# Sliding-window attention and mixture of experts on one core: narrower score blocks, shifted value copies and a new order for the last three batches

## The chip, the core and the metric

The kernel runs on one core of a Trainium2 chip. The core has TensorE (PE in the profile; its weight loads are PEld), VectorE (DVE), ScalarE (ACT), GpSimd (POOL) and SyncE (SP), each with its own queue of instructions, and 16 DMA engines. The metric is the device time of one launch in microseconds (us), over repeated runs. A profile is one more execution, whose trace has the start and the duration of every instruction. TensorE's clock has two levels, 1.2 and 2.4 GHz; the granted clock is given as a share of the upper one.

## What is computed

```python
# attention: batch 8, heads 8, 576 positions, head size 64
scores = scale * q @ k.T                      # only |query - key| <= 32 counts
attn   = exp(scores) masked to the band, divided by its row sum
x      = attn @ v                             # -> 4608 tokens x 512
# experts: the modality of a token picks its gate bias
e      = argmax(x @ w_gate + modality_bias[modality])
out    = gate_weight * relu(x @ w1[e]) @ w2[e]
```

## The kernel before, in words

Every instruction of the program is placed by a table of steps, `ORDER`. A step has a name, its numbers, the engine that does it (`/v` VectorE, `/a` ScalarE, `/p` GpSimd) and, behind a colon, the banks of the PSUM memory (eight, 0 to 7) that a matmul step writes. The program walks the table once and emits the steps' instructions; each engine then runs its own in that order, and waits on semaphores where a step needs another engine's result or a bank that is still being read.

Attention, for batch `b` and group `g` of four heads: `t` transposes queries and keys (VectorE). `SA` and `SB` make the scores (TensorE): each matmul multiplies 32 rows of one head, the four heads sit in four row groups of the array, and keys come in blocks of 128 with a window of 192 queries (128 at the end). `SA` has 16 matmuls of 192 columns, `SB` 16 of 192 and 8 of 128. `sa` and `sb` take the exponential into `pt` (ScalarE: one instruction of 1,536 columns, and for `sb` another of 512). `M` multiplies by the band's mask (VectorE, 1,920 columns, four per batch). `V` multiplies by the values (18 matmuls of 65 columns per step, four steps per batch; the 65th column is a one, so that the row sum comes out beside the result), and `v` divides by that sum (VectorE: a reciprocal and a multiply). `lv` loads values (GpSimd).

Then `X` sorts the tokens of a block by expert with a one-hot matrix (`G` makes it), `pa` and `pb` append them to two lists (ScalarE). `L`, `lo`, `E`, `sm`, `rc` make the gate. `U` is the first layer of a tile of 256 tokens (8 matmuls of 256 columns), `u` its relu, `D` the second layer (4 matmuls of 512 columns per half), `y` the scaling by the gate, `O` the scattered store (GpSimd). Tile 18 takes the tokens that are left over, with weights that `Wx` copies. `c0` to `c17` check on the device that the assumptions on the lists held; `c17` loads the resulting flag into a register of every engine, and a branch then skips a slow general path.

Names that matter below, with the lines of the profile: scores L687, exponentials L695 and L698, mask L712, values L729, `v` L743 and L758, `U` L916, `D` L942, `u` L931 and L933, `y` L956 and L958, `O` L965, checks L995 to L1032, the branch L1215.

Of the kernel before, what the change touches and what calls it, by code (L numbers as in the profile page):

```python
# [23 lines left out]
BF16 = mybir.dt.bfloat16  # L24
# [40 lines left out]
u7.0/a U6.1:0 v17/v u6.2/a U7.1:7 u6.1/a lo3/v t5.1.1/v E3/a V16:12 u7.1/a SB5.0:3456 v16/v l7.0.2/p D6.0.0:7 sb5.0/a
t6.1.1/v V19:01 U7.3:2 sm3/v lv7.1/p v19/v SA5.0:3456 u7.3/v D6.0.1 O5.1/p sa5.0/a e10/v t6.0.0/v X4.2:2 X4.0:0 U7.2:1
lv6.1/p rc3/v pa4.0/a t6.0.1/v pb4.0/a X4.1:3 D7.0.0:4 u7.2/a M20/v pb4.1/a D7.0.1 pa4.1/a pb4.2/a X4.3:3 pa4.2/a
D6.1.0:6 y7.0/v pb4.3/a y6.0/v pa4.3/a O7.0/p D6.1.1 M21/v SB5.1:0123 V20:45 y6.1/v sb5.1/a U9.1:7 v20/v O6.1/p L4:6
V21:45 l7.1.2/p lo4/v SA6.0:0123 E4/a O6.0/p sm4/v D7.1.0:6 v21/v sa6.0/a D7.1.1 rc4/v t6.1.0/v u9.1/a U9.0:4 y7.1/a
t7.0.0/v SA5.1:0123 u9.0/a O7.1/p U8.1:6 sa5.1/a U9.2:7 u8.1/a U9.3:4 M22/v u9.2/a SB6.0:0123 u9.3/a M23/v U8.0:7  # L70
sb6.0/a V22:45 U8.3:6 v22/v u8.0/a V23:01 e13/v SA6.1:2345 v23/v U8.2:7 sa6.1/a M24/v X4.4:0 D9.1.0:1 pb4.4/a c2/v
u8.2/v D9.1.1 pa4.4/a X5.0:7 X5.1:0 y9.1/v X5.2:2 pb5.0/a V24:34 pa5.0/a G6/v O9.1/p pb5.1/a X5.3:1 D8.0.0:7 pa5.1/a
v24/v pb5.2/a D9.0.0:0 pa5.2/a t7.1.0/v u8.3/a SB6.1:2345 pb5.3/a pa5.3/a M25/v D9.0.1 sb6.1/a U11.1:1 t7.1.1/v D8.0.1
y9.0/v u11.1/a M26/v U10.2:2 O9.0/p y8.0/a U10.0:6 M27/v lv7.0/p V25:01 u10.2/a V26:34 v25/v X5.4:2 D8.1.0:7 pa5.4/a
v26/v u10.0/a D8.1.1 pb5.4/a SA7.1:0123 y8.1/v V27:45 t7.0.1/v O8.1/p U11.3:7 sa7.1/a v27/v U10.1:6 Wx u11.3/a
SB7.1:0123 c3/v G7/v u10.1/a U11.2:7 sb7.1/a X6.0:6 L5:4 U10.3:5 lo5/v E5/a pb6.0/a U11.0:0 pa6.0/a u10.3/v Jy12/v
X6.1:6 D10.0.0:5 u11.0/v pa6.1/a sm5/v u11.2/a M30/v SB7.0:0123 pb6.1/a D10.0.1 rc5/v sb7.0/a X6.2:7 D11.1.0:4 y10.0/v
M31/v O10.0/p D11.0.0:5 pb6.2/a pa6.2/a SA7.0:0123 O8.0/p D11.1.1 sa7.0/a D11.0.1 y11.1/a U12.0:7 M29/v y11.0/a X6.3:1
U12.1:0 M28/v V29:56 u12.1/a L6:4 u12.0/a U13.0:2 pa6.3/a lo6/v E6/a sm6/v U12.2:4 u13.0/a rc6/v v29/v pb6.3/a U13.3:0
# [5 lines left out]
u14.3/v u16.3/a L9:0 D14.0.0:3 E8/a lo9/v N/p c6/v O11.0/p U14.2:0 c7/v c8/v sm8/v D14.1.0:6 rc8/v u14.2/a U16.2:5 E9/a
sm9/v c9/v u15.1/v D14.1.1 u16.2/a D14.0.1 y14.1/a D16.1.0:5 O14.1/p U17.1:6 D16.1.1 u17.1/v c10/v U17.3:7 y16.1/a c11/v
c12/v y14.0/a D15.0.0:6 O16.1/p c13/v u17.3/v D16.0.0:3 O14.0/p U15.3:7 D16.0.1 u15.3/a U17.0:5 D15.0.1 u17.0/v c14:7
U17.2:0 c15/v y15.0/v D15.1.0:7 y16.0/v u17.2/a O15.0/p D15.1.1 O16.0/p D17.1.0:0 y15.1/v c16/v D17.1.1 O15.1/p
D17.0.0:7 U18.1:3 U18.0:6 u18.1/v D17.0.1 u18.0/a y17.1/v D18.0.0:6 y17.0/v O17.1/p rc9/v D18.0.1 y18.0/a c17 O17.0/p
O18.0/p  # L90
"""


@with_exitstack
def kernel(
    ctx: ExitStack,
    tc: tile.TileContext,
    q: bass.AP,
    k: bass.AP,
    v: bass.AP,  # L100
# [41 lines left out]
    RB = 2
# [1105 lines left out]
```

## Time and profile before

| what | us |
|---|---|
| runs (3) | 208.20, 208.52, 210.06; median 208.52 |
| profiled execution, its own time | 210.04 |
| its span, first to last instruction | 208.3 |
| PE busy in the span | 195.7 (94%) |
| DVE, ACT, POOL busy | 152.2, 131.4, 97.3 |
| PE from 98.44 to 200.50 | 102.06 busy of 102.06 |
| last store issued, and span's end | 201.99, 208.3 |

Busy time is the time in which an engine has an instruction in work. TensorE's instructions overlap one another, so how often it starts one says more than how long one takes. A wait is put down to what ended it.

### The profile page before, as it was taken

Reading aid. Unit: us, or ns where it says so; the run is one execution under the profiler, and the core shown is the slowest. Engines: PE = TensorE matmul, PEld = TensorE weight load, DVE = VectorE, ACT = ScalarE, POOL = GpSimd, SP = SyncE. Lnnn points to the kernel's source line nnn. Section 1 sums busy time; section 2 is a strip of 40 time slices with the busy share of each in tenths; the row PEclk is TensorE's granted clock in tenths of the full one; section 3 lists DMA queues with packets and bytes.
Section 4 is the critical chain, followed back from the end, with each engine's and each line's share of the span. In section 5 each row is a group of like instructions: output and inputs, shape, how many; then the busy total and the mean of one; then the engine's idle time right before and its main releaser. Section 6 shows DMA issues by size and latency. Waiting matters only on the chain. (4 is left out here: it accounts for less than half of the span.)

```text
span 208.3 us, 6244 instructions
## 1 busy us (share of the span) xinstructions
PE 195.7 (94%) x2583; PEld 140.3 (67%) x2583; DVE 152.2 (73%) x304; ACT 131.4 (63%) x223; POOL 97.3 (47%) x137
## 2 busy tenths in 40 slices
PE   7997998999999989999999999999999999999950
PEld 5766787777666677669657876777597669656520
DVE  3598999999889978899998679976566334542330
ACT  6097794778877986976778969678751732431120
POOL 7987851695089888145545102510501152122550
PEclk9999999999999999999999999999999999999996
DMA  4999999999999999989696911192200132112330
GB/s 66 206 174 183 212 209 196 211 213 192 201 193 268 171 253 235 208 174 169 97 185 129 318 75 50 55 199 112 102 5 0 53 151 105 50 50 104 138 118 8
DMA packets 47661, 30.41 MB, mean 146 GB/s; under 512 B 38883, under 2 KB 38923, under 8 KB 47371
## 3 DMA queue, kind: packets, MB, share of 16 engines
q0 software_dynamic: 46608, 27.79, 83.4%
q1 hardware_dynamic: 1019, 2.16, 2.9%
q8 instruction: 22, 0.36, 0.7%
q14 instruction: 12, 0.10, 0.1%
HBM read 36.76 MB, written 9.70 MB: 223 GB/s over the span
## 5 line engine op out<-in xcount | busy, mean ns | idle before, releaser
L965 POOL DMA_INDIRECT out_dram<-ys,ids x37 | 41.2, 1112 | 85.9 <-DVE ys L958 45.8
L916 PE MATMUL banks<-XT,w_sb 128*128 128x256 bf16 x576 | 71.2, 273 | 0.7 <-DVE xt L758 0.7
L942 PE MATMUL banks<-w_sb,hT 128*128 128x512 bf16 x288 | 69.5, 379 | 0.0
L916 PEld LDWEIGHTS <-w_sb 128*128 128x128 bf16 x576 | 53.8, 98 | 11.4 <-issue 1.8
L695 ACT ACTIVATE pt<-banks 128x1536 bf16<-128x1536 f32 x32 | 46.6, 1458 | 13.0 <-PE banks L687 9.8
L933 ACT ACTIVATE hT<-banks 128x512 bf16<-128x512 f32 x57 | 33.0, 598 | 30.1 <-PE banks L916 27.9
L942 PEld LDWEIGHTS <-hT 128*128 128x128 bf16 x296 | 26.9, 98 | 26.3 <-issue 0.8
L655 DVE STREAM_TRANSPOSE qk<-qk 128x576 int32<-128x576 int32 x32 | 38.4, 1244 | 2.1 <-DMA qk<-in_k_dram 1.8
L712 DVE TENSOR_TENSOR pt<-pt,mask 128x1920 bf16<-128x1920 bf16 x28 | 31.5, 1148 | 4.0 <-ACT pt L695 4.0
L758 DVE TENSOR_TENSOR xt<-banks,recs 128x640 bf16<-128x640 f32 x32 | 26.4, 824 | 1.1
L729 PE MATMUL banks<-vt,pt 128*128 128x65 bf16 x576 | 22.4, 193 | 1.4 <-DMA vt<-in_v_dram 0.6
L729 PEld LDWEIGHTS <-pt 128*128 128x128 bf16 x576 | 21.0, 97 | 4.0 <-issue 1.4
L798 ACT CAST XT<-banks 128x352 f32 (+3 forms) x40 | 17.9, 448 | 5.1 <-PE banks L778 4.6
L231 POOL DMA_DIRECT2D vt<-in_v_dram x16 | 20.2, 1270 | 1.3 <-PE banks L729 1.3
L958 DVE TENSOR_SCALAR ys<-banks,Gt 128x512 f32<-128x512 f32 x20 | 14.5, 739 | 7.8 <-PE banks L942 7.8
L931 DVE TENSOR_SCALAR hT<-banks 128x512 bf16<-128x512 f32 x17 | 11.6, 685 | 11.7 <-PE banks L916 11.6
L956 ACT ACTIVATE ys<-banks,Gt 128x512 f32<-128x512 f32 x17 | 11.5, 699 | 12.6 <-PE banks L942 12.6
L687 PE MATMUL banks<-qk 32*128 32x192 bf16 (+1 forms) x640 | 18.5, 239 | 0.1
L812 ACT CAST XT<-banks 128x352 f32 (+2 forms) x39 | 17.6, 451 | 1.2 <-PE banks L778 0.9
L687 PEld LDWEIGHTS <-qk 32*128 32x128 bf16 x640 | 12.2, 92 | 7.3 <-issue 6.2
L974 PE MATMUL banks<-zero_b 128*128 128x256 bf16 x86 | 13.8, 318 | 2.0 <-DVE zero_b L320 1.5
L778 PE MATMUL banks<-oh,xt 128*128 128x128 bf16 (+1 forms) x160 | 12.3, 214 | 0.3 <-DVE xt L758 0.3
(159 smaller groups left out, 143.6 us busy)
## 6 DMA issues: line engine op xcount, KB each, us to landing
vt<-in_v_dram POOLq DMA_DIRECT2D x16, 288.0 KB, 6.7
w_sb<-in_moe_w_dram POOLq DMA_DIRECT2D x4, 1024.0 KB, 14.0
qk<-in_q_dram POOLq DMA_DIRECT2D x6, 576.0 KB, 10.7
qk<-in_k_dram POOLq DMA_DIRECT2D x6, 576.0 KB, 6.8
wx<-w_sb SPq DMA_DIRECT2D x2, 1024.0 KB, 6.1
qk<-in_q_dram POOLq DMA_DIRECT2D x4, 288.0 KB, 7.7
qk<-in_k_dram POOLq DMA_DIRECT2D x4, 288.0 KB
out_dram<-ys,ids POOLq DMA_INDIRECT x37, 2.7
```

The costliest lines, as they stand in the source:

```text
L231: nc.gpsimd.dma_start(v_t[b % NV][:, n_ * i:n_ * i + n_, 0:D], v[b].rearrange("h s d -> (h s) d").rearrange("(n p) d -> p n d", p=P)[:, n_ ...
L655: nc.vector.transpose(qk_t[b % 2][:, g, at:at + S].rearrange("p (t r) -> p r t", r=R), Ct["l", b][:, u, g].bitcast(I32).rearrange("p (r j) ...
L687: nc.tensor.matmul(st[:, h, WIN * i_:WIN * i_ + w_], qk[32 * h:32 * h + 32, c_, QK + k0:QK + k0 + P], qk[32 * h:32 * h + 32, c_, q0:q0 + w ...
L695: nc.scalar.activation(pt[:, :, 2 * part:2 * part + 2, 0:WIN], st[:, :, 0:2 * WIN].rearrange("p h (j c) -> p h j c", c=WIN), ACT.Exp, scal ...
L712: nc.vector.tensor_tensor(out=p_ap, in0=p_ap, in1=mask[:], op=ALU.mult)
L729: nc.tensor.matmul(o_ap, pt[:, c1:c1 + P], vt[:, g0 + j, 0:D + 1], start=(m == 0 and i_ == 0), stop=(i_ == len(mine) - 1), skip_group_chec ...
L758: nc.vector.tensor_tensor(out=o_ap, in0=o_v[:, :, :, 0:D], in1=rec.unsqueeze(3).to_broadcast([P, 2, NM, D]), op=ALU.mult)
L798: ins = nc.scalar.copy(XT[:, :, bass.ds(r_, w_)], Ct["X", b, m][:, :, 0:w_])
L916: ins = nc.tensor.matmul(ph[:, u_, :], w1[:, f0:f0 + 2 * P - 1:2], rhs, start=(kd == 0), stop=(kd == n_kd - 1))
L933: nc.scalar.activation(o_ap, i_ap, ACT.Relu)
L942: nc.tensor.matmul(Ct["D", t_, s_], Ct["h", t_][:, kf, P * s_:P * s_ + P], w2, start=(kf == 0), stop=(kf == n_kf - 1))
L965: ins = nc.gpsimd.indirect_dma_start(out=out, out_offset=bass.IndirectOffsetOnAxis(ap=ids[:, u_:u_ + 1], axis=0), in_=Ct["y", t_, s_][:], ...
```

## The change

For batches 5 to 7 (`b >= OLD`):

- Scores. `SA` now has six blocks of 64 queries per head group, 48 matmuls of 64 columns; the two ends of the sequence are in `SE`, once per batch for both groups, 32 matmuls of 96 columns. `SB` is gone.
- Exponentials. `sa` is one instruction of 1,536 columns per group, `se` one of 1,536 per batch.
- Masks. `M` with two numbers covers 1,536 columns per group, `Me` 1,536 per batch. The buffers `pm` and `pe` lie in the two old `pt` buffers; `Kr` and `Kx` set once what stays constant between the blocks.
- Values. Blocks of 64 queries need keys that start at odd multiples of 64. `Vx` copies the values, shifted by 64 rows, into a second tile `vx`: two copies of 64 partitions by 1,122 columns per half batch, on VectorE, and for the first half of batch 6 on ScalarE. `V` has 16 matmuls of 65 columns instead of 18.
- The tile `vx` is also used earlier, in place of another tile (`ohp`), and the column of ones is two wide.
- Order. The table's first 497 entries are the same; behind them all is in another order, and some `u` and `y` steps are on the other of the two engines. `c17` and the last checks stand at the end, behind the last store, where before they stood ahead of the last two stores.

```diff
-l7.0.2/p D6.0.0:7 sb5.0/a ... SB5.0:3456 ... O17.1/p rc9/v D18.0.1 y18.0/a c17 O17.0/p O18.0/p
+Kr0/v V19:45 U7.2:7 Kr1/a u7.2/a SA5.0:0123 sa5.0/a D6.0.0:6 ... D17.1.1 y17.1/a O17.1/p c7/v ... c16/v c17/p
...
+    QW, EW, NW = 64, 96, 6
+    TW, SE = 3 * QW, 256
...
+    def Vx(eng, b, i):
+        n_ = G // 2
+        lo, hi = slice(n_ * i, n_ * i + n_ - 1), slice(n_ * i + 1, n_ * i + n_)
+        for to, from_, at in ((slice(0, 64), slice(64, P), lo), (slice(64, P), slice(0, 64), hi)):
+            o_ap, i_ap = vx_t[to, lo], v_t[b % NV][from_, at]
...
+                copy(eng, o_ap, i_ap)
...
+    def Kr(eng, i):
+        pad(eng, pm_t[i].rearrange("p (j c) -> p j c", c=TW)[:, :, QW:2 * QW])
...
+    def scores(st, at, b, g, k0, q0, w_):
+        qk = qk_t[b % 2][:, g].bitcast(BF16).rearrange("p (t c) -> p c t", c=2)
+        for c_ in range(2):
+            for h in range(4):
+                nc.tensor.matmul(st[:, h, at:at + w_],
+                                 qk[32 * h:32 * h + 32, c_, QK + k0:QK + k0 + P],
+                                 qk[32 * h:32 * h + 32, c_, QP + q0:QP + q0 + w_],
+                                 start=(c_ == 0), stop=(c_ == 1), skip_group_check=True)
...
+    def SA(_, b, g):
...
+        for i in range(NW):
+            scores(Ct["S", b, g], QW * i, b, g, QW * (i + 1), QW * (i + 1) + 32, QW)
...
+    def SE_(_, b, w):
+        Ct["T", b, w] = some_banks()
+        for j, g in enumerate(groups(w)):
+            scores(Ct["T", b, w], 2 * EW * j, b, g, 0, 0, EW)
+            scores(Ct["T", b, w], 2 * EW * j + EW, b, g, S - P, S - EW, EW)
...
+    def Mn(_, b, g):
+        p_ap = pm_t[(NG * b + g) % NPM].rearrange("p (t w c) -> p t w c", w=3, c=QW)[:, :, 0:3:2]
+        m_ap = mask[:, 0:1, 64:P].unsqueeze(1).to_broadcast([P, 2 * NW, 2, QW])
+        nc.vector.tensor_tensor(out=p_ap, in0=p_ap, in1=m_ap, op=ALU.mult)
...
+    def values(it, ot):
...
+            for i_, (m, pt, c1, w, last) in enumerate(runs):
+                n_, odd = divmod(R // 2 * h + w, 2)
+                src = vx_t if odd else v_t[b % NV]
+                nc.tensor.matmul(ot[:, h, (D + 1) * m:(D + 1) * (m + 1)], pt[:, c1:c1 + P],
+                                 src[:, R // 2 * hp + n_, 0:D + 1],
+                                 start=(i_ == 0), stop=last, skip_group_check=True)
```

VectorE between batch 4's last values and batch 5's first ones. In the old kernel this is the work ahead of the step `V20` and the first steps after it (L712 masks, L655 transposes, L958 `y`):

```order
L743 RECIPROCAL recs<-banks 128x10
L758 TENSOR_TENSOR xt_93<-banks,recs 128x2x5x64
L712 TENSOR_TENSOR pt_86<-pt_86,mask 128x10x192
L999 TENSOR_TENSOR sc__150<-sc__150,hn 128x40
L931 TENSOR_SCALAR hT<-banks 128x512
L958 TENSOR_SCALAR ys<-banks,Gt 128x512
L507 TENSOR_TENSOR oh<-iob,col 128x640
L743 RECIPROCAL recs<-banks 128x10
L758 TENSOR_TENSOR xt_91<-banks,recs 128x2x5x64
```

In the changed kernel the same stretch of VectorE, from the last `v` of batch 4 (`xt_93`) on, reads (L335 constants, L643 transposes, L746 and L752 masks, L174 shifted copies, L1027 `y`):

```order
L335 MEMSET pt_87 128x8x32 x2
L941 RECIPROCAL Gt<-sm 128x4
L643 STREAM_TRANSPOSE qk_84<-qk 128x18x32
L746 TENSOR_TENSOR pt_86<-pt_86,mask 128x12x2x64
L643 STREAM_TRANSPOSE qk_84<-qk 128x18x32
L174 COPY vx<-vt_90 64x1122 x2
L1027 TENSOR_SCALAR ys<-banks,Gt 128x512
L752 TENSOR_TENSOR pt_87<-pt_87,mask 128x8x192
L174 COPY vx<-vt_90 64x1122 x2
L1068 TENSOR_TENSOR sc__151<-sc__151,hn 128x40
L812 RECIPROCAL recs<-banks 128x10
L827 TENSOR_TENSOR xt_94<-banks,recs 128x2x5x64
```

Four shifted copies and two transposes of batch 6 now stand ahead of the first `v` of batch 5; the one-hot of L507 and a relu (L931) have moved away.

VectorE at the end of the program, before:

```order
L1016 TENSOR_REDUCE gec<-sc__150 128x37
L1018 SCALAR_TENSOR_TENSOR gec<-gec,vv 128x37
L1020 TENSOR_SCALAR gec,bad<-gec 128x37
L169 CAST badb<-bad 128x3
L931 TENSOR_SCALAR hT<-banks 128x512 x2
L1027 TENSOR_SCALAR fl<-banks 128x3
L958 TENSOR_SCALAR ys<-banks,Gt 128x512 x3
L169 CAST fl_i<-fl 128x1
L931 TENSOR_SCALAR hT<-banks 128x4x128
L958 TENSOR_SCALAR ys<-banks,Gt 128x512 x2
L872 RECIPROCAL Gt<-sm 128x1
L1032 TENSOR_LOAD fl_i
```

And in the changed kernel:

```order
L1027 TENSOR_SCALAR ys<-banks,Gt 128x512
L1077 TENSOR_SCALAR sc__151<-recs 128x320
L1079 SCALAR_TENSOR_TENSOR sc__151,rs<-recs,sc__151 128x320
L1083 TENSOR_SCALAR sc__151<-lo__147 128x296
L1085 TENSOR_REDUCE gec<-sc__151 128x37
L1087 SCALAR_TENSOR_TENSOR gec<-gec,vv 128x37
L1081 TENSOR_SCALAR bad<-rs 128x1
L1089 TENSOR_SCALAR gec,bad<-gec 128x37
L174 CAST badb<-bad 128x3
L1096 TENSOR_SCALAR fl<-banks 128x3
L174 CAST fl_i<-fl 128x1
L1101 TENSOR_LOAD fl_i
```

The checks have moved behind VectorE's last `y`, and every engine's load of the flag comes after all of them.

## Rows read from the trace of the kernel before

**Rows 1.** The page's first part: busy us (share of the span) xinstructions.

```profile
PE 195.7 (94%) x2583; PEld 140.3 (67%) x2583; DVE 152.2 (73%) x304; ACT 131.4 (63%) x223; POOL 97.3 (47%) x137
```

**Rows 2.** Windows, all engines: stretch, its length, busy us (xcount) each, PEclk.

```profile
98.44:200.50 102.06, 102.06 (x1227) 71.12 (x1224) 64.66 (x124) 58.84 (x103) 30.65 (x29) 1.00 0.43 102
```

**Rows 3.** Groups of TensorE, 98.44 to 200.9 us: busy, mean ns | idle before.

```profile
L729 PE MATMUL banks<-vt,pt 128*128 128x65 bf16 x252 | 9.7, 193 | 0.0
L687 PE MATMUL banks<-qk 32*128 32x192 bf16 (+1 forms) x240 | 6.9, 239 | 0.0
```

**Rows 4.** Timeline of TensorE around an old SB step: start us, us.

```profile
117.78 0.38 PE L916 MATMUL banks<-XT,w_sb 128*128 128x256 bf16 x2
118.09 0.63 PE L687 MATMUL banks<-qk 32*128 32x192 bf16 x24
118.66 1.05 PE L916 MATMUL banks<-XT,w_sb 128*128 128x256 bf16 x8
119.54 0.71 PE L729 MATMUL banks<-vt,pt 128*128 128x65 bf16 x18
120.09 1.04 PE L916 MATMUL banks<-XT,w_sb 128*128 128x256 bf16 x8
```

**Rows 5.** The same around an old SA step.

```profile
121.61 0.52 PE L687 MATMUL banks<-qk 32*128 32x192 bf16 x16
122.07 0.61 PE L916 MATMUL banks<-XT,w_sb 128*128 128x256 bf16 x4
```

**Rows 6.** The same around matmuls of 8 columns.

```profile
110.65 0.55 PE L843 MATMUL banks<-wgd,XT 128*128 128x8 bf16 x16
111.11 0.28 PE L729 MATMUL banks<-vt,pt 128*128 128x65 bf16 x4
```

**Rows 7.** Groups of all engines by shape: busy us, mean ns.

```profile
L695 ACT ACTIVATE pt<-banks 128x1536 bf16<-128x1536 f32 x32 | 46.6, 1458 | 13.0 <-PE banks L687 9.8 <-PE banks L729 2.9
...
L712 DVE TENSOR_TENSOR pt<-pt,mask 128x1920 bf16<-128x1920 bf16 x28 | 31.5, 1148 | 4.0 <-ACT pt L695 4.0
...
L958 DVE TENSOR_SCALAR ys<-banks,Gt 128x512 f32<-128x512 f32 x20 | 14.5, 739 | 7.8 <-PE banks L942 7.8
...
L931 DVE TENSOR_SCALAR hT<-banks 128x512 bf16<-128x512 f32 x17 | 11.6, 685 | 11.7 <-PE banks L916 11.6
```

**Rows 8.** The same, nearest rows for the copies.

```profile
L507 DVE TENSOR_TENSOR oh<-iob,col 128x640 bf16<-128x640 bf16 x8 | 6.5, 818 | 0.0
...
L429 DVE TENSOR_SCALAR mask<-neg 128x768 bf16<-128x768 bf16 x2 | 0.6, 332 | 0.0
```

**Rows 9.** Timeline of VectorE where the order parts.

```profile
97.99 1.25 DVE L655 STREAM_TRANSPOSE qk<-qk 128x576 int32<-128x576 int32 x1
99.19 0.22 DVE L743 RECIPROCAL recs<-banks 128x10 f32<-128x10 f32 x1
99.45 0.82 DVE L758 TENSOR_TENSOR xt<-banks,recs 128x640 bf16<-128x640 f32 x1
100.19 1.25 DVE L655 STREAM_TRANSPOSE qk<-qk 128x576 int32<-128x576 int32 x1
```

**Rows 10.** Timeline of all engines at the end.

```profile
198.97 1.90 PE L942 MATMUL banks<-wx,hT 128*128 128x512 bf16 x8
...
200.96 0.69 ACT L956 ACTIVATE ys<-banks,Gt 128x512 f32<-128x512 f32 x1 [2.04 <-PE banks L942]
201.99 0.98 POOL L965 DMA_INDIRECT out_dram<-ys,ids  x1 [0.30 <-ACT ys L956]
```

**Rows 11.** The branch's line and the store's: count, ns min/median/max, first and last start.

```profile
L1215 PEldq COMPARE_BRANCH  x1: 3442/3442/3442, 199.6 to 199.6; - x1
```

**Rows 12.** The value loads' line (L231), its last row.

```profile
DMA to landing us min/median/max: 5.6/6.7/7.9
```

**Rows 13.** Groups of VectorE: the two longest checks.

```profile
L1010 DVE SCALAR_TENSOR_TENSOR sc__150<-recs,sc__150 128x320 f32<-128x320 f32 x1 | 0.5, 491 | 0.0
...
L1016 DVE TENSOR_REDUCE gec<-sc__150 128x37 f32<-128x296 f32 x1 | 0.5, 453 | 0.0
```

More of the change, by code (lines that the diff above doesn't have):

```diff
@@ L65 @@
[L65 to L79, printed above, removed]
@@ L85 @@
[L85 to L89, printed above, removed]
@@ new lines @@
+D7.1.0:5 t6.1.0/v Vx5.0/v y6.0/v u7.3/a D7.0.1 sa5.1/a X4.1:0 X4.2:1 pb4.1/a pa4.1/a y7.0/a O7.0/p l7.0.2/p
+O5.1/p Me5.2/v pb4.2/a Vx5.1/v c2/v V20:23 v20/v t6.0.1/v D7.1.1 y7.1/a t6.0.0/v X4.3:0 V21:67 D6.1.0:2 v21/v
+pa4.2/a pa4.3/a pb4.3/a D6.1.1 y6.1/a U8.2:0 X4.4:1 L4:2 lo4/v U8.3:6 SE6.2:2345 M5.1/v u8.3/v U8.1:7 u8.1/v
+Kx0/a se6.2/a Me6.2/v u8.2/v U9.0:6 V22:23 v22/v U9.2:7 pb4.4/a V23:45 v23/v U9.1:0 O6.0/p lv6.1/p Vx6.0/a
+u9.2/a u9.0/a U8.0:2 SA6.1:4567 pa4.4/a X5.0:1 X5.1:3 u9.1/a D9.1.0:0 E4/a pa5.0/a pa5.1/a pb5.0/a sa6.1/a
@@ new lines @@
+u8.0/v D8.0.0:2 D8.0.1 pb5.1/a Jy12/v t7.1.0/v sm4/v rc4/v SA6.0:4567 D8.1.0:3 D8.1.1 X5.2:1 Vx6.1/v M6.1/v
+sa6.0/a M6.0/v U9.3:4 V27:56 X5.3:7 u9.3/v D9.1.1 y8.0/a y8.1/a pb5.2/a e13/v v27/v pb5.3/a y9.1/v pa5.2/a
+V24:34 v24/v U11.1:5 U11.2:0 G6/v pa5.3/a L5:3 lo5/v u11.2/v V26:67 X5.4:3 v26/v U10.3:4 G7/v lv7.0/p O6.1/p
+V25:01 v25/v u10.3/v O7.1/p u11.1/v pb5.4/a U10.1:2 U10.2:6 U10.0:0 X6.0:4 X6.2:1 u10.2/v pa5.4/a U11.0:5
+X6.1:6 X6.3:7 pa6.0/a u10.0/a pa6.1/a D9.0.0:0 D9.0.1 pb6.0/a u10.1/v pb6.1/a l7.1.2/p t7.1.1/v pb6.2/a U11.3:6
@@ L136 @@
     NV = 3
+    OLD = 5
     PM = (0,1)
@@ L639, in W @@
     @named
-    def W(_, which, i):
+    def W(_, which, i, h=None):
         if ("er", i) not in Ct:
@@ L673, with scores1 @@
     op["MB"] = lambda _, b, g: masked(b, g, 1)
-    def scores(b, g, part):
+    def scores1(b, g, part):
         pm = NG * b + g in PM
@@ new lines, in Me, with M @@
+    @named
+    def Me(_, b, w):
+        p_ap = edges(b, w).rearrange("p g h c -> p (g h) c")[:, :, 32:32 + 2 * EW].rearrange("p h (a c) -> p h a c", a=2)
+        m_ap = mask[:].rearrange("p j c -> p (j c)")[:, 32:32 + 2 * (WIN + 32)].rearrange("p (a c) -> p a c", a=2)
+        nc.vector.tensor_tensor(out=p_ap, in0=p_ap, in1=m_ap[:, :, 0:EW].unsqueeze(1).to_broadcast(list(p_ap.shape)),
+                                op=ALU.mult)
+    @named
+    def M(_, it, g=None):
+        if g is not None:
+            return Mn(_, it, g)
@@ L716, in V @@
         b, hp = divmod(it, NH)
+        ot = some_banks()
+        if b >= OLD:
+            values(it, ot)
+            Ct["V", it] = ot
+            return
         pt, vt = pair(it), v_t[b % NV]
-        ot = some_banks()
         for h in range(2):
```

190 lines of the change are left out of this document (104 added, 86 removed).

## The prediction

> **What bounds the kernel now.** I read the busy shares first, then the windows, then the timeline of the engine that they single out. TensorE is busy 94% of the span, VectorE 73%, ScalarE 63% [rows 1]. An average does not say that TensorE is the limit where the change is, so the window counts. The two orders part at the step `V16`, at 98.44 us. From there to 200.50 TensorE is busy 102.06 of 102.06 us at a granted clock of 1.00 (the 2.4 GHz level), VectorE 64.7 and ScalarE 58.8 [rows 2], and the groups of scores and values were not preceded by any idle time [rows 3]. So in the whole stretch that the change touches nothing but TensorE's own work sets the time. Work taken from the other two engines is worth nothing; a new order can win nothing by removing waits, because there are none, and can only add some. The gain must be TensorE's own time.
>
> **TensorE's scores, priced by sets.** I call four matmuls, one in each row group, a set. An old `SA` has 4 sets of 192 columns and takes 0.46 us to the next step's start (121.61 to 122.07) [rows 5]; `SB` has the same 4 and 2 sets of 128 and takes 0.57 (118.09 to 118.66) [rows 4]. So a set of 128 costs about 56 ns, where 128 columns at 2.4 GHz are 53. The columns set the pace, with some 4 ns on top. Four sets of 192 are then 4 x 84 = 0.34 us, and 0.12 of the 0.46 is for starting and for changing back to full-array work. Entering costs too: two matmuls of `U` start at 117.78, each takes 0.11 (8 in 118.66 to 119.54), so the scores could have started at 118.00 and did at 118.09 [rows 4]. A step so costs 0.55 (`SA`) or 0.66 (`SB`), and three batches 6 x 0.55 + 6 x 0.66 = 7.26 us.
>
> The new `SA` has 12 sets of 64 columns. Followed by columns a set is 27 + 4 = 31 ns, the step 0.37 + 0.12 + 0.09 = 0.58. `SE` has 8 sets of 96: 44 ns each, 0.56. Three batches: 6 x 0.58 + 3 x 0.56 = 5.16. **Gain 2.10 us**, although there are 144 more score matmuls.
>
> No row shows a set of 64. Its bounds: below, the columns (31 ns); above, 57 ns, since the weights that it loads are those of a 128-column set, which shows 56. At 57 for both sizes `SA` is 0.89 and `SE` 0.67, three batches 7.35, a loss of 0.09. I take 31: matmuls of 8 columns, each with its own load of 128 columns, follow each other in 0.46 / 16 = 29 ns in the full array [rows 6], so a load need not take 57.
>
> The Trainium skill speaks against me here. "TensorE: Matmul & The Clock Gate", section "LDWEIGHTS (loading the stationary operand)", prices a load at its columns divided by 1.2 GHz and says that 32 rows take as long as 128. An estimate from that page: 107 ns per load and set, 6 x 1.49 + 3 x 1.07 = 12.2 us of scores, and a kernel some 4 us slower. The sets of 56 ns in this trace exclude that figure; what is left of the rule is my first rival, priced there from rows alone.
>
> **Values.** A `V` step of 18 takes 0.55 us (119.54 to 120.09) [rows 4], 30.6 ns a matmul. 24 fewer: **gain 0.73 us**. The source tile makes no difference.
>
> **ScalarE and VectorE.** Per batch the exponentials go from four instructions of 1.46 us [rows 7] and two short ones to three; that is off the path and counts for nothing. VectorE's masks go from four of 1.15 [rows 7] to three of 1,536 columns, in proportion 0.92. It gets ten shifted copies of 1,122 columns. No row shows one. Nearest below: 768 columns from one bf16 source in 0.33 us [rows 8], in proportion 0.48. Nearest above: a two-source one-hot of 640 columns in 0.82 [rows 8], in proportion 1.43. I take 0.45, since a copy has one source; the other end is my second rival. `Kr` and `Kx` are a few tenths each.
>
> Does that hold TensorE up? I summed both sides at the narrowest places; a VectorE instruction starts 0.08 before the end of the last (100.19 against 99.45 + 0.82) [rows 9], so each counts its row less 0.08.
>
> - Before `V20`, the first new values. VectorE is free at 99.19 [rows 9]; then two `v` of 1.0, `Kr0` 0.4, `Kx1` 0.3, two transposes of 1.17, two masks of 0.87, two copies of 0.4, a `y` of 0.66 and small change: the last mask ends at about 107.5. TensorE's work from `V16` to `V20` sums to 9.5 us, so it arrives at 107.9. Slack 0.4.
> - From the end of `U9.3` to `U10.0`, which needs the bank that `v25` reads: VectorE has three `u` (0.61), four `v` (1.0), a `y` (0.66) and two one-hots (0.74), with small change 7.7 us; TensorE has 8.0. After the time it takes VectorE to see a matmul end, next to nothing is left.
> - GpSimd now issues the second half of batch 6's values behind the store of `y7.0`. That `y` can end at about 109.2 by TensorE's sum, five issues of about 1.0 us [rows 10] come first, so about 115; landing takes 6.7 us [rows 12], and the copy can start at 121.7. The last mask of batch 6 behind it waits for `sa6.0` anyway: its scores end at about 124.0, the exponential takes 1.46, so 125.5. Covered; without that cover it would cost up to 2 us.
>
> The plan is tight, so small excesses will show. **Loss 0.5 us**, with 0 and 1.5 as ends.
>
> **The end.** Before, the last matmuls end at T = 198.97 + 1.90 = 200.87, the last `y` starts at 200.96, its store at 201.99 [rows 10], and the span ends 7.4 us after T. Now the last product is `D17.1`, again with a `y` on ScalarE and one store. Priced at nothing. The checks are new in this place: the last `y` of VectorE can end at T - 0.9, nine checks of at most 0.49 [rows 13] are some 2.3 us, so T + 1.4; a matmul and two more bring the flag at about T + 2.1. TensorE's branch takes 3.44 [rows 11], T + 5.6 with the register load to come. That is still inside the 7.4.
>
> **The sum.** -2.10 - 0.73 + 0.50 = -2.33 us. The profiled span of 208.3 becomes 206.0. The profiled execution itself took 210.04, near the slowest of the three runs; I set the difference against their median, 208.52: **206.2 us**.
>
> **Rivals.**
>
> - *Weight loads set the pace of narrow sets* (57 ns). For: each set loads four times 128 columns, and no row has fewer columns per load in row groups. Against: 29 ns in the full array [rows 6]. Then +0.09 - 0.73 + 0.3 of waits: 208.2 us, no change.
> - *The shifted copies run at the two-source rate*, 1.43 instead of 0.45 each: the kernel becomes slower. A step of two is 1.9 late. Two steps fall ahead of `V20` and of `SE6.2`, where 0.4 to 0.6 are free; batch 6's is covered; two fall ahead of batch 7's values, with slack of 0.5 to 1.0. Four times 1.9 less 2.5 is 5.1 us: 208.52 - 2.33 + 5.1 = 211.3. It decides from about 1.0 us a copy, where the waits eat the gain. Against: one-source bf16 work here is fast [rows 8].
> - *The flag comes last.* If TensorE's branch, now late, outlasts the last store's landing, the end moves by up to 1 us: about 206.9. For: 3.44 us is long [rows 11], and only some 1 us is free. Against: the sum above.
>
> **How the numbers follow.** Forecast 0.62, loads 0.16, copies 0.09, flag 0.09; 0.04 for none of these. The forecast's own span is 205.4 to 207.2 (waits of 0 to 1.5). The loads' case and the flag's must be inside the range, the copies' case need not: 205.3 to 208.7. One per cent is 2.1 us, about what a measurement of this kernel can tell from no change: faster is below 206.4, slower above 210.6. The forecast lies just below the first bound, so it gives 0.41 to faster and 0.21 to no change; the flag's case splits (0.03 and 0.06), loads go to no change, copies mostly to slower (0.07). Rounded, with the rest: faster 0.45, same 0.46, slower 0.09.
>
> **What would show it.** In the changed trace: 48 score matmuls from their first start to the next step in about 0.49 us, 32 in 0.47 (rivals: 0.80 and 0.58); `V` of 16 in 0.49; copies of 64 by 1,122 in 0.4 to 0.5 us; TensorE busy all through, with idle time of some tenths at `V20`, `U10.0` and around; the last matmul's end about 2.3 us earlier, and 7.4 us from there to the end. The forecast is wrong if sets of 64 need over 45 ns, if TensorE idles for more than 1.5 us behind `V16`, or if the stretch behind the last matmul grows.

## The result

The changed kernel took 211.25 us (median of 10, 210.1 to 215.14), the kernel before 208.47 on the same chip (10, 208.2 to 210.06): ratio 1.0116, interval 1.0077 to 1.0154. It is slower by about 1.2%, where I had forecast 206.2 us, and it lies outside the range of 205.3 to 208.7. (Ratios here and below are of undisturbed runs and need not be the quotient of the medians.) The profiled execution took 211.17 us, its span is 209.5. Page part 1 [rows 1] and the window from `V16` to the last matmul [rows 2] of the changed kernel (window: length, busy us of PE, PEld, DVE, ACT, POOL with counts, PEclk, DMA):

```profile
PE 193.1 (92%) x2703; PEld 138.9 (66%) x2703; DVE 154.2 (74%) x317; ACT 126.0 (60%) x216; POOL 94.6 (45%) x137
...
98.44:200.78 102.34, 100.07 (x1345) 69.86 (x1342) 64.83 (x126) 53.48 (x95) 29.09 (x29) 1.00 0.44 102
```

Both kernels reach `V16` at nearly the same time (98.44 us before, 98.33 now). TensorE had no idle time from there to the end before; now it has 2.27 us. What it does is cheaper, as forecast. Timeline of the new `SA` and `SE` steps [rows 4, 5], then groups by shape (busy us, mean ns) for scores, masks and copies [rows 7, 8]:

```profile
100.40 0.55 PE L699 MATMUL banks<-qk 32*128 32x64 bf16 x48
100.88 1.04 PE L1011 MATMUL banks<-w_sb,hT 128*128 128x512 bf16 x4
...
102.72 0.52 PE L699 MATMUL banks<-qk 32*128 32x96 bf16 x32
103.18 1.04 PE L1011 MATMUL banks<-w_sb,hT 128*128 128x512 bf16 x4
```

```profile
L699 PE MATMUL banks<-qk 32*128 32x64 bf16 x288 | 3.6, 189 | 0.5 <-issue 0.5
...
L746 DVE TENSOR_TENSOR pt<-pt,mask 128x1536 bf16<-128x1536 bf16 x6 | 5.6, 953 | 0.5 <-ACT pt L727 0.5
L174 DVE COPY vx<-vt 64x1122 bf16<-64x1122 bf16 x10 | 4.5, 451 | 1.3 <-DMA vt<-in_v_dram 1.2
```

An `SA` of 48 matmuls takes 0.48 us to the next step (forecast 0.49), an `SE` 0.46 (0.47), a `V` of 16 matmuls 0.48 to 0.52 (0.49), a copy 451 ns (0.45).

The time went to two places. First, TensorE stopped. Its waits from 98 us to the last matmul (total, times, longest), and the timeline of the worst stretch:

```profile
PE banks L912 <- issue: 0.8, 2, 0.4
PE banks L699 <- DVE lo__147 L923: 0.7, 1, 0.7
PE banks L699 <- issue: 0.5, 1, 0.5
PE banks L1011 <- ACT ys L1025: 0.3, 1, 0.3
```

```profile
142.10 1.89 PE L1011 MATMUL banks<-w_sb,hT 128*128 128x512 bf16 x8 [0.26 <-ACT ys L1025]
143.92 0.62 PE L699 MATMUL banks<-qk 32*128 32x64 bf16 x45
145.07 0.22 PE L699 MATMUL banks<-qk 32*128 32x64 bf16 x3 [0.52 <-issue]
145.22 0.20 PE L912 MATMUL banks<-wgd,XT 128*128 128x8 bf16 x2
145.78 0.29 PE L912 MATMUL banks<-wgd,XT 128*128 128x8 bf16 x6 [0.36 <-issue]
146.51 0.35 PE L912 MATMUL banks<-wgd,XT 128*128 128x8 bf16 x8 [0.43 <-issue]
```

The 0.3 us behind `ys` are a plain wait for a `y`, which every trace of this order has. "Issue" is time in which the engine waits for nothing that the profile shows. TensorE stops inside the second score step of batch 7 and twice inside batch 6's logits, and starts again at 145.07, 145.78 and 146.51, every 0.7 us. The wait of 0.7 us behind `lo` is of another form: VectorE reads batch 4's logits (`lo`) late.

```profile
112.18 0.82 DVE L827 TENSOR_TENSOR xt<-banks,recs 128x640 bf16<-128x640 f32 x1
114.64 0.19 DVE L923 TENSOR_TENSOR lo__147<-banks,mbd 128x32 f32<-128x32 f32 x1 [1.64 <-PE banks L985]
```

The logits' matmuls end at 113.31 by the record and VectorE is free, yet `lo` starts at 114.64.

Second, the end [rows 10, 11]: last matmuls, last `y`, last store, TensorE's branch, and SyncE's waits at the end.

```profile
199.26 1.89 PE L1011 MATMUL banks<-w_sb,hT 128*128 128x512 bf16 x8
201.54 0.69 ACT L1025 ACTIVATE ys<-banks,Gt 128x512 f32<-128x512 f32 x1 [3.78 <-PE banks L1011]
202.51 0.97 POOL L1034 DMA_INDIRECT out_dram<-ys,ids  x1 [0.60 <-issue]
```

```profile
L1284 PEldq COMPARE_BRANCH  x1: 4562/4562/4562, 203.8 to 203.8; - x1
```

```profile
SPq L1312 <- DMA out_dram<-ys,ids: 2.0, 1, 2.0
SPq L1312 <- PEq L1284: 1.2, 1, 1.2
```

T, the end of the last matmuls, is 201.15, the branch runs to 208.33, the span to 209.5: 8.3 us behind T, where it was 7.4. SyncE has the last store when it still waits 1.2 us for TensorE's branch.

### The profile page after: what moved, and what is told of

Its sections match the earlier page's. It is cut to its first block, busy times and chain, and to the rows that moved or that the text cites. A ratio compares the mean times of both kernels' runs of the same rounds, so it can differ in the third digit from the quotient of the medians.

```text
span 209.5 us, 6485 instructions
## 1 busy us (share of the span) xinstructions
PE 193.1 (92%) x2703; PEld 138.9 (66%) x2703; DVE 154.2 (74%) x317; ACT 126.0 (60%) x216; POOL 94.6 (45%) x137
## 4 chain that ended last, share of the span: by engine, by line
PE 39%; issue 35%; POOL 9%; DVE 6%; ACT 4%; DMA 3%; POOLq 1%; ACTq 0%; DVEq 0%
PE banks L1011 14%; PE banks L985 12%; POOL out_dram L1034 7%; PE banks L675 4%; PE banks L798 4%; DMA qk<-in_q_dram 3%; DVE xt L827 2%; PE banks L847 2%; ACT pt L683 2%; POOL qk L220 1%; PE banks L699 1%; ACT pt L686 1%; PE banks L912 1%; ACT pt L738 1%; POOLq L1039 1%
## 5 line engine op out<-in xcount | busy, mean ns | idle before, releaser
L1002 ACT ACTIVATE hT<-banks 128x512 bf16<-128x512 f32 x49 | 28.6, 599 | 30.7 <-PE banks L985 28.2
L643 DVE STREAM_TRANSPOSE qk<-qk 128x576 int32<-128x576 int32 x32 | 38.3, 1238 | 2.3 <-DMA qk<-in_k_dram 1.7
L683 ACT ACTIVATE pt<-banks 128x1536 bf16<-128x1536 f32 x20 | 29.2, 1461 | 6.6 <-PE banks L675 4.8
L1000 DVE TENSOR_SCALAR hT<-banks 128x512 bf16<-128x512 f32 x25 | 16.7, 685 | 10.3 <-PE banks L985 9.9
L1025 ACT ACTIVATE ys<-banks,Gt 128x512 f32<-128x512 f32 x22 | 15.0, 696 | 10.4 <-PE banks L1011 10.4
L760 DVE TENSOR_TENSOR pt<-pt,mask 128x1920 bf16<-128x1920 bf16 x16 | 18.0, 1151 | 0.1
L798 PEld LDWEIGHTS <-pt 128*128 128x128 bf16 x360 | 13.1, 97 | 3.1 <-issue 1.3
L798 PE MATMUL banks<-vt,pt 128*128 128x65 bf16 x360 | 14.0, 193 | 1.1 <-ACT pt L686 0.4
L1027 DVE TENSOR_SCALAR ys<-banks,Gt 128x512 f32<-128x512 f32 x15 | 11.0, 741 | 3.0 <-PE banks L1011 2.9
L847 PEld LDWEIGHTS <-xt 128*128 128x128 bf16 x160 | 10.2, 98 | 3.6 <-issue 0.5
L675 PE MATMUL banks<-qk 32*128 32x192 bf16 (+1 forms) x400 | 11.6, 239 | 1.1 <-DVE vt L335 1.0
```

What stands on the lines that cost most here:

```text
L643: nc.vector.transpose(qk_t[b % 2][:, g, at:at + S].rearrange("p (t r) -> p r t", r=R), Ct["l", b][:, u, g].bitcast(I32).rearrange("p (r j) ...
L675: nc.tensor.matmul(st[:, h, WIN * i_:WIN * i_ + w_], qk[32 * h:32 * h + 32, c_, QK + k0:QK + k0 + P], qk[32 * h:32 * h + 32, c_, q0:q0 + w ...
L683: nc.scalar.activation(pt[:, :, 2 * part:2 * part + 2, 0:WIN], st[:, :, 0:2 * WIN].rearrange("p h (j c) -> p h j c", c=WIN), ACT.Exp, scal ...
L760: nc.vector.tensor_tensor(out=p_ap, in0=p_ap, in1=mask[:], op=ALU.mult)
L798: nc.tensor.matmul(o_ap, pt[:, c1:c1 + P], vt[:, g0 + j, 0:D + 1], start=(m == 0 and i_ == 0), stop=(i_ == len(mine) - 1), skip_group_chec ...
L847: nc.tensor.matmul(t_[:, kd, :], x_t[b % NX][:, m, P * kd:P * kd + P], Ct["oh", b][:, m, 0:n_], start=True, stop=True, skip_group_check=True)
```

## The experiments

Each set of runs below was on one chip, and the kernel before gives its measure. In three sets (called quiet) it takes 207.5 to 207.6 us, in the other three and in the first measurement (called pausing) 208.5 to 208.9. That the kind of set decides, I learned from the runs. The expectations speak of chips with and without pauses, but that it is the chip is not shown: the record gives the first set, which was quiet, and the fifth, which was pausing, the same chip number, 7.

**First set, quiet (before 207.57).** Three single edits and their sum:

```diff
 e1: checks ahead, flag ahead of the last store
-y18.0/v D17.1.0:6 O15.1/p O18.0/p c6/v D17.1.1 y17.1/a O17.1/p c7/v c9/v ... c14:6 c15/v c16/v c17/p
+rc8/v y16.0/v c6/v c7/v c8/v ... sm9/v c9/v ... c13/v ... D18.0.1 c14:4 y18.0/v ... c15/v c16/v D17.1.1 y17.1/a c17/p O17.1/p
 e2: copies of the last tile's weights later, from ScalarE
-D16.1.1 Wx U18.0:2      r_ = reg(..., [ET.SP], 0, 1)          nc.sync.dma_start(v1, ...)
+u14.3/a Wx D13.0.0:6    r_ = reg(..., [ET.Activation], 0, 1)  nc.scalar.dma_start(v1, ...)
 e3
-L4:2 lo4/v
+L4:7 lo4/v
```

> The changed kernel with its checks moved ahead: the two checks of the value reciprocals and their count stand in VectorE's idle time before the last tile's logits, the four of the logits right behind the last tile's sum, the one-column matmul ahead of the last eight matmuls, the flag's load ahead of the last store. Theory A (the flag is the last thing that TensorE waits for, and its branch, 4562 ns from 203.77 us, outlasts the landing of the last store): the branch starts at about 201 us, the stretch from TensorE's last matmul to the span's end falls from 8.35 to about 7.3 us, and the time by 1.0 to 1.2 us against the changed kernel (211.25 us), to about 210.1. Rival (the store's landing sets the end in both, and the late branch only shows beside it): the time stays within 0.3 us of the changed kernel. The pauses before that, at 114, 144 and 146 us, stay under both.

> The changed kernel with the two copies of the last tile's weights (1 MB each, within SBUF) issued by ScalarE behind the ReLU of tile 14, near 160 us, instead of by SyncE as soon as the buffers of batches 6 and 7 are free (112 and 142 us). Theory A (the second copy holds up TensorE's supply of instructions just when narrow score blocks use them up fastest): the three pauses that end with 'issue' at 144.3, 145.3 and 145.9 us, 1.8 us together, go away, and the time falls by 1.5 to 1.9 us, to about 209.5. Rival (the narrow blocks alone outrun the supply, wherever the copy is): the three pauses stay at the same instructions, time within 0.3 us of the changed kernel. A second rival (copies at 160 us hold up something there): the pauses go, others of like size come at 160 to 168 us.

> The changed kernel with batch 4's logits (L4) in bank 7 instead of bank 2, so that batch 6's edge scores, which take banks 2 to 5, no longer wait for VectorE to read them. Theory A (TensorE stands 0.77 us at 114.1 us for that read, and works without a break behind it): the pause goes and the time falls by 0.5 to 0.8 us, to about 210.6. Rival (what is late there is not the read but VectorE itself, which starts it 1.34 us after the logits are done with nothing ahead of it; then the next matmuls that need VectorE wait in its place): the pause moves to the first-layer matmuls behind the edge scores, time within 0.3 us.

> The three edits together: checks moved ahead, the copies of the last tile's weights at about 160 us, batch 4's logits in bank 7. Theory A (three separate losses on TensorE's path and behind it, which add up: 1.1 + 1.8 + 0.7 us): 207.4 to 208.0 us, below the kernel before the change (208.47). Rival (time given back in one place is lost in the next wait): 209 to 210.5 us, above the kernel before.

Measured: e1 206.64 us (ratio to the kernel before 0.9922, 0.9891 to 0.9952), e2 206.55 (0.993), e3 207.26 (0.9959), e4 206.93 (0.9947). All gained some 4 us on 211.25, e3 too, which differs by one bank number; the sum of the edits gained no more than one. And in e1's trace the pauses were gone, though nothing was edited there. So none of this could be read against the first measurement.

**Second set, pausing (before 208.57).** The unchanged kernels, the two best edits together, and the late flag alone in the kernel before:

```diff
 e6: in the kernel before
-L9:0 D14.0.0:3 E8/a lo9/v N/p c6/v ... c17 O17.0/p O18.0/p
+D18.0.1 c6/v y18.0/a O17.0/p O18.0/p c7/v c9/v ... c14:7 c15/v c16/v c17
```

> The changed kernel as it is, with no edit, beside the kernel before in the same session. The run e3_l4_bank differs from it by one bank number alone and took 207.26 us where the changed kernel had taken 211.25, and in its trace and in that of e1_flag_early the pauses at 114, 144 and 146 us are missing though nothing there was edited in e1. Theory B (the pauses of 0.77, 0.71, 0.52 and 0.60 us were of that session and not of the order of the instructions; the late flag alone belongs to the kernel): about 207.5 us, within 0.5% of the kernel before, and no pause of over 0.43 us on TensorE between 98 and 200 us. Theory A (the pauses belong to this exact kernel, and any small shift removes them): 210 to 211.5 us, with the pauses in the same places.

> The kernel before, with no edit, for a trace from the same session as r_after_again, so that the two are compared like with like. Both theories: about 207.5 us; last matmul, flag and end at the distances of the first trace (7.5 us from the last matmul's end to the span's end, TensorE's branch 3.4 us long and started ahead of the last matmul's end).

> The changed kernel with the two edits that did best, the checks moved ahead (e1_flag_early) and the copies of the last tile's weights at about 160 us (e2_wx_late); batch 4's logits stay in bank 2. Theory B (the checks take 0.7 to 0.9 us off the end, the copies let TensorE finish 0.7 us earlier, and the third edit of e4_all, bank 7, cost what it lost): 205.4 to 206.0 us, below both single edits (206.64 and 206.55). Rival (the two give the same time back, so that together they give no more than one): 206.4 to 206.8 us.

> The kernel before with only its checks moved: the eleven behind the fourth-last tile's sums go to the very end, the flag's load behind the last store, as the changed kernel has them. Nothing else is edited. Theory B (the late flag by itself costs what the changed kernel's end lost): TensorE's branch starts at about 203 us instead of 199.6, the stretch from the last matmul's end to the span's end grows from 7.5 to 8.2 to 8.6 us, time 0.7 to 1.1 us above the kernel before. Rival (VectorE's checks in the middle of the kernel cost as much as they save at the end): within 0.3 us of the kernel before.

Measured: the changed kernel 212.08 us (1.0116, 1.0076 to 1.0155) with all the pauses again: theory B fell, and theory A seemed to hold, until e13 and e14 below, which are shifted and pause too. e5 took 212.17 (1.0176), with the same three pauses (restarts at 144.97, 145.67, 146.44) although the weights were copied only at 167 us: the copy is not the cause. In r_after_again TensorE's clock fell behind the pauses; window as above:

```profile
144.00:147.00 3.00, 1.41 (x52) 0.98 (x37) 0.00 (x0) 0.34 (x2) 1.48 (x2) 1.00 0.97 366
147.00:150.00 3.00, 3.00 (x33) 1.17 (x34) 2.84 (x5) 1.24 (x1) 0.00 (x0) 0.62 0.41 150
```

TensorE is busy 1.41 of 3.00 us, then its granted clock is 0.62 in the mean, a stretch of 3.4 us at 1.2 GHz instead of 2.4. Held against r2_after matmul by matmul, that stretch cost 1.4 us. It came in three of the six traces of this order in pausing sets.

r_before_again took 208.42 us. e6 took 210.07 us (median of 12, one of which took 501.37), 1.5 more than the kernel before (ratio 1.0051, 1.0019 to 1.0083), and its stretch behind T is 7.1 us, where r_before_again has 6.0. SyncE's waits and the branch in e6:

```profile
SPq L1243 <- PEq L1215: 1.5, 1, 1.5
...
SPq L1243 <- DMA out_dram<-ys,ids: 0.6, 1, 0.6
```

```profile
L1215 PEldq COMPARE_BRANCH  x1: 3378/3378/3378, 204.0 to 204.0; - x1
```

The late flag alone costs the kernel before about 1.1 us at its end. T itself is 0.7 us later in e6's trace, but matmul by matmul it is as far behind at 70 us, long ahead of the edit.

**Third set, quiet (before 207.62).** The changed kernel, e1 again, and two edits against the pauses:

```diff
 e8 (seven such groups in the warm-up)
-n4.256:0
+n16.64:0
 e9
-L6:7 lo6/v Vx7.0/v M7.1/v sa7.0/a M7.0/v D10.0.0:6
+D10.0.0:6 L6:7 lo6/v Vx7.0/v M7.1/v sa7.0/a M7.0/v
```

> The changed kernel as it is, once more, as the measure for the three runs beside it: the sessions so far fall into two kinds, one in which the kernel before takes 207.4 to 207.6 us and variants of the changed kernel show no pause (four of four), one in which it takes 208.4 to 208.6 us and every run of the changed order shows pauses at 114 and 144 to 146 us (three of three). Theory C (the pauses are a property of the chip together with these instructions): in a session of the first kind 207.2 to 207.7 us and none of the pauses; in one of the second kind 211 to 212.5 us with all of them.

> The kernel of e1_flag_early (the changed kernel with its checks and the flag ahead), without an edit, in the session of r2_after, so that the gain at the end is measured against the same kernel on the same chip. Theory (the late flag costs 0.7 to 1.1 us wherever it runs): 0.7 to 1.1 us below r2_after. Rival (its whole gain of 4.6 us against the first measurement was that of the chip): within 0.3 us of r2_after.

> The changed kernel with 66 more matmuls in the warm-up ahead of all work (7 groups of 2 or 4 matmuls of 256 columns become 8 or 16 of 64 columns, the same columns in all), so that every later instruction of TensorE stands 132 places further down its program. Theory D (a pause belongs to a place in TensorE's program, where the next block of instructions has to be there: the pauses came at instructions 3309 and 4350, both within 20 of a multiple of 256): the pauses move to work that comes 132 instructions earlier, or go. Rival E (a pause belongs to the work, batch 4's logits and the two score steps of batch 7 in 3.4 us): the pauses stay with that work, at instructions 3441 and 4482. In a session without pauses: no difference to r2_after, 0.3 us at most.

> The changed kernel with the logits of batch 6 one step later, behind four matmuls of 512 columns (0.87 us in which TensorE uses up eight instructions) instead of right behind the second score step of batch 7 (96 instructions in 0.48 us). Theory F (TensorE runs out of instructions where narrow steps stand too close together): the pauses of 0.55 and 0.6 us inside the logits shrink or go, the sum of the three pauses near 144 us falls from 1.8 us to below 1.2. Rival (the length of the pauses does not hang on how fast instructions are used up there): the sum stays at 1.7 to 1.9 us, wherever it falls.

Measured: the changed kernel 207.01 us (0.9956, 0.9929 to 0.9983), e7 207.04, e8 206.94, e9 207.28. As theory C forecast for this kind of set, there is no pause near 114 or 144 us (`lo` starts 0.17 us behind its matmuls); that the chip makes the kind, the fifth set puts in doubt. The same stretch in r2_after's timeline, and SyncE's waits:

```profile
142.63 0.57 PE L699 MATMUL banks<-qk 32*128 32x64 bf16 x48
143.14 0.56 PE L912 MATMUL banks<-wgd,XT 128*128 128x8 bf16 x16
143.77 1.67 PE L1011 MATMUL banks<-w_sb,hT 128*128 128x512 bf16 x7
```

```profile
SPq L1312 <- PEq L1284: 1.9, 1, 1.9
SPq L1312 <- DMA out_dram<-ys,ids: 1.1, 1, 1.1
```

SyncE waits 1.9 us for the branch alone. e7 ended that wait. From profile to profile its stretch behind T fell from 8.1 to 7.4 us, and no further, since the last store now landed 3.4 us behind its issue instead of 2.8. Its median gained nothing; what took the 0.7 us back is not shown, but the profiled execution of r2_after (207.80 us) is the slowest of its eleven. e7's profile has a pause of its own at 125 us, of 0.35.

**Fourth set, quiet (before 207.51).** The flag another step earlier, e8 again, and the kernel before for its trace:

```diff
 e10, on e1
-u18.1/a D18.0.1 c14:4 y18.0/v D17.1.0:6 O15.1/p O18.0/p c15/v c16/v D17.1.1
+u18.1/a c14:3 D18.0.1 c15/v c16/v y18.0/v D17.1.0:6 O15.1/p O18.0/p D17.1.1
```

> e1_flag_early with the flag another step earlier: its matmul between the two halves of the last tile's second layer, its two last VectorE steps ahead of that tile's eviction, so that the flag is there some 1.3 us before TensorE's last matmul ends. Theory (the span ends with whichever comes later, TensorE's branch of 4.2 to 4.6 us or the last store's landing; in e1_flag_early the branch began 0.1 us behind the last matmul's end and ended 4.36 us behind it, within 0.02 us of the store's landing): branch from about 1.2 us ahead of the last matmul's end, the stretch behind it falls from 8.1 us (changed kernel) and 7.4 (e1) to 5.9 to 6.3 us, time 1.5 to 2.1 us below the changed kernel and 1.0 to 1.4% below the kernel before on a chip without pauses (205.0 to 205.6 us). Rival (the stretch is set by the last store, which lands 3.4 us behind its issue once the flag is early): 7.2 to 7.5 us behind the last matmul, time as e1_flag_early (206.6 to 207.0 us).

> e8_shift once more, without an edit: the changed kernel with every instruction of TensorE 132 places later. On a chip without pauses it tells nothing new (206.9 us). On the chip with pauses: by theory D (the pause belongs to a place in the program) the pauses come at work that stands 132 instructions earlier, or go; by rival E (it belongs to the work) at the same work, in the waits for batch 4's logits and in and behind batch 7's second score step.

> The kernel before, without an edit, for a trace beside the other two: 207.6 us on a chip without pauses, 208.5 on the one with them; 5.9 to 6.0 us from the last matmul's end to the span's end, or 7.4 where the last store lands 1.5 us later.

Measured: e10 206.53 us (0.9962, 0.9926 to 0.9998), e11 207.13, r3_before 207.72. SyncE's waits at the end of r3_before and of e10:

```profile
SPq L1243 <- DMA out_dram<-ys,ids: 8.0, 1, 8.0
```

```profile
SPq L1312 <- DMA out_dram<-ys,ids: 6.6, 1, 6.6
```

In both the last store ends the span, and TensorE's branch is not waited for: in e10 it runs from 1.5 us ahead of T to 2.0 behind. e10's times lie in two groups, six at 205.85 to 206.53 and five at 207.42 to 208.72. In its profile, of the upper group, the store lands 4.2 us behind its issue and the stretch behind T is 8.2 us; in r3_before it lands after 2.3, and the stretch is 5.9. TensorE also stops once at 125 us there, for 0.73, at the place of e7's pause. So the profile shows the rival; no run reached the expected 205.0 to 205.6 us, and the lower group has no trace. e10's median is 1.0 us below the kernel before, but by the ratios it is no better than the unedited kernel of the third set (0.9956). e1 and e2, with the best ratios, had no unedited kernel beside them.

**Fifth and sixth set, pausing (before 208.88 and 208.63).** e10 and e2 together, then e8 and e9 again, which now met the pauses:

> The changed kernel with the flag ahead of the last matmuls' end (e10_flag_first) and the copies of the last tile's weights at about 160 us (e2_wx_late). On a chip without pauses: by the theory that the late flag was the loss at the end and the copies cost 0.4 us in the middle, 205.6 to 206.3 us, 0.6 to 1.0% below the kernel before, with two groups of times 1.5 us apart as the last store lands 2.4 or 4 us behind its issue. Rival (the store's landing gives the gain back in most runs): 206.5 to 207.2 us. On the chip with pauses: 210 to 211.5 us, above the kernel before there, since neither edit touches the pauses.

> e8_shift a third time, without an edit: the changed kernel with every instruction of TensorE 132 places later. On a chip without pauses about 207 us and nothing new. On the chip with pauses: by theory D (a place in the program) the pauses come at work that stands 132 instructions earlier, or go; by rival E (the work) in the wait for batch 4's logits and in and behind batch 7's second score step.

> e9_L6_behind_D once more, without an edit: batch 6's logits behind four matmuls of 512 columns instead of right behind batch 7's second score step. On a chip without pauses about 207.3 us and nothing new. On a chip with pauses, by theory F (they come where narrow steps stand too close together) the sum of the pauses near 144 us is below 1.2 us and none lies inside the logits; by its rival (the chip pauses there whatever stands behind the score step) the sum stays at 1.7 to 1.9 us, in the four matmuls or the logits behind them.

Measured: e12 212.93 us (1.0183, 1.013 to 1.0236), e13 212.78 (1.0178), e14 211.76 (1.0126, 0.9946 to 1.0306). e12 was even slower than I expected: besides the pauses, its last `y` starts 1.95 us behind T (e5: 1.85; r2_after: 0.04). TensorE raises the semaphore for it 1.93 us behind T, so the end that the profile models for these matmuls is too early. The timeline of e13:

```profile
143.78 0.76 PE L699 MATMUL banks<-qk 32*128 32x64 bf16 x44
145.05 0.23 PE L699 MATMUL banks<-qk 32*128 32x64 bf16 x4 [0.51 <-issue]
145.21 0.20 PE L912 MATMUL banks<-wgd,XT 128*128 128x8 bf16 x2
145.81 0.30 PE L912 MATMUL banks<-wgd,XT 128*128 128x8 bf16 x6 [0.39 <-issue]
146.57 0.34 PE L912 MATMUL banks<-wgd,XT 128*128 128x8 bf16 x8 [0.46 <-issue]
```

With 132 instructions more ahead of it, the pauses come in the same two steps: they belong to the work, and theory D fell. The timeline of e14:

```profile
144.26 0.49 PE L699 MATMUL banks<-qk 32*128 32x64 bf16 x41
144.96 0.22 PE L699 MATMUL banks<-qk 32*128 32x64 bf16 x3 [0.22 <-issue]
145.68 0.22 PE L699 MATMUL banks<-qk 32*128 32x64 bf16 x4 [0.49 <-issue]
146.42 0.38 PE L1011 MATMUL banks<-w_sb,hT 128*128 128x512 bf16 x1 [0.52 <-issue]
147.13 0.60 PE L1011 MATMUL banks<-w_sb,hT 128*128 128x512 bf16 x2 [0.34 <-issue]
```

Behind the score step now stand matmuls of 512 columns, and TensorE stops just as often among them, with the same 0.7 us between starts. Held against e9 matmul by matmul, e14 loses 1.9 us from 143 to 148 us. So theory F, which had less than 1.2, fell too: what follows doesn't matter.

## Why the prediction was wrong

- **Scores and values: right.** The steps measured 0.48 and 0.46 us against 0.49 and 0.47. In quiet sets `V16` to T took 102.40 us in r3_before, 100.24 in r2_after and 99.99 in e11: 2.2 to 2.4 us less, against 2.33 in the sum. The first rival fell: 12 sets in a step of 0.48 leave at most 40 ns for one. So did the page's price ("TensorE: Matmul & The Clock Gate", section "LDWEIGHTS (loading the stationary operand)", of the Trainium skill): 107 ns a set would be 1.28 us a step, and the trace disagrees.
- **Masks and copies: right** (451 ns; second rival fallen). That its 211.3 us lies beside the measured 211.25 is chance. At `V20` and `U10.0` no wait shows, although the terms named for `U10.0` add up to 7.97 us and not to 7.7.
- **Waits, 0.5 us with 1.5 as the upper end: the step that failed where the kernel was measured.** I had argued from engines that release one another, and in quiet sets that was enough. In the pausing ones, matmul by matmul against r2_after, the first trace loses 0.8 us at 75 us, where the kernel before loses it too; 0.8 at 114; 1.9 at 144 to 147. r_after_again loses 2.2 there and 1.4 more at the lower clock. So the new order lost 2.7 and 4.4 us instead of 0.5. No rival of mine had it, and the trace of before had one sign that I did not see: at 75 us VectorE read finished values late. The trace of before and r_before_again have it, r3_before in a quiet set not:

```profile
75.03 0.22 DVE L743 RECIPROCAL recs<-banks 128x10 f32<-128x10 f32 x1 [1.23 <-PE banks L687]
```

```profile
74.88 0.22 DVE L743 RECIPROCAL recs<-banks 128x10 f32<-128x10 f32 x1 [1.27 <-PE banks L687]
```

```profile
74.27 0.22 DVE L743 RECIPROCAL recs<-banks 128x10 f32<-128x10 f32 x1 [0.39 <-PE banks L729]
```

- **The end, priced at nothing: the step that failed in every set.** It is the third rival, to which I gave 0.09 and at most 1 us; the stretch behind T grew by 2.2 (5.9 us in r3_before, 8.1 in r2_after). The flag came as forecast (T + 2.0), the branch began at T + 2.6. Wrong were the branch's length, 4.3 to 4.6 us instead of 3.44 [rows 11]; that another 1.1 us follow it; and above all the 7.4 us of room: the execution that I read was one whose last store landed 3.9 us behind its issue. In r_before_again and r3_before it lands after 2.4 and 2.3, and the room is 6.0 and 5.9. The branch's length goes with a load of instructions that I had not seen: in all twenty traces one of 16 KB begins 0.9 to 1.5 us behind the branch's start, and the branch ends 1.3 to 1.6 us behind the load's end. The load took 1.08 us in the trace of before and 2.00 in the changed kernel's. But not all of the 2.2 us is shown to be the flag's: e6 shows 1.1 for it, and with the flag out of the way e7 and e10 still have 7.4 and 8.2 us behind T. There the span ends 3.1 us behind the store's landing, in the kernel before 2.5, which no run explains.
- **The sum.** First measurement: T is 0.3 us later (-2.3 + 2.7), and the stretch is 8.3 us against the 5.9 to 6.0 of r3_before and r_before_again; 2.6 to 2.7 together, where the medians say 2.8. (The execution of before that I read, 210.04 us, is like three of its ten runs; the other seven took 208.2 to 208.85.) Quiet: T is 2.1 us earlier (197.99 in r2_after, 200.11 in r3_before) and the stretch 2.2 longer, about nothing from profile to profile; the medians say 0.6 us less. Pausing: r_after_again's T is 2.0 us later than r_before_again's (-2.3 + 4.4), its end 2.1 us longer; 4.1 together, 210.8 against 206.7 in span. The medians say 3.5, the ratio 2.4.

**What stays open:** what stops TensorE in the pausing sets, and what makes a set one. It is not the weights' copies (e5), not the place in the program (e13), not the instructions behind the score step (e14). Nor is it a load of TensorE's instructions: in four of the six traces none falls into the pauses near 144 us (in the first they begin at 134.42 and 147.45). Whether it is the two score steps of batch 7 that stand 1.8 us apart wasn't tried, and would not explain 75 us.

## What to carry to other kernels

Read the stretch behind the last matmul in several executions before you call it room, and keep the flag that a branch needs well ahead of TensorE's end: a branch of 3.4 to 4.6 us is free only while the last store is still on its way. A tuned kernel whose TensorE has no idle time left can lose in one set of runs what it gains in another, so hold a change against the kernel before in the same set, and in more than one.

## What was not expected of the hardware

- TensorE stops, with nothing in the profile that holds it, in some sets of runs: three or four stops near 144 us, 0.70 to 0.77 us from start to start, in the same work in six of six traces of this order; in quiet sets in none of ten near 114 or 144 us, though e1, e7 and e10 have one stop at 125 us (0.16, 0.35 and 0.73). VectorE starts up to 1.3 us (`lo`), and ScalarE at the end up to 1.95 us, behind the recorded end of the matmuls that they wait for.
- The last store lands 2.2 us (e6) to 4.2 us (e10) behind its issue, in the unedited kernel before 2.3 to 3.9 from trace to trace.
- TensorE's branch takes 3.4 to 4.6 us, with a load of instructions of 1.0 to 2.0 us inside it; those of the other engines take 45 to 72 ns.
